# Transposed tokens through one PSUM bank, a third bank for the first layer, and a larger lead for routing steps: a mixture-of-experts kernel

## Chip, cores and metric

The kernel runs on one core of a Trainium2 chip. The metric is device time in microseconds (us), the median of three runs. Everything is one launch: a short causal convolution, the routing of its rows to eight experts, and the experts' two-layer networks.

## What is computed

```python
# x (8, 3584, 192) f32, weight (8, 7); w_gate (192, 8), w1 (8, 192, 1024), w2 (8, 1024, 192)
attn = 7-tap causal convolution of x along the sequence, one softmaxed filter per 24 channels
x = attn.reshape(28672, 192);  cap = 28672 // 8
logits = x @ w_gate
for idx in np.argsort(-logits.flatten()):     # greedy: best (token, expert) pairs first
    ...                                       # a token takes its first expert with room (cap 3584)
for e in range(8):
    mask = assigned == e
    out[mask] = np.maximum(x[mask] @ w1[e], 0.0) @ w2[e]
```

All data are float32. The kernel multiplies in float32r and splits an operand into a rounded part ("hi", names ending in h) and the rest ("lo", names ending in l), and adds the products that matter.

## The kernel before

**Stages.** Up to about 205 us the kernel computes the convolution in 16 pieces, the logits, and a first threshold. From then to the end it runs the experts' networks in `FFN.run`, one tile of 512 tokens after another, 56 tiles in all. Routing isn't finished when the experts start: the first 8 tiles (one per expert) hold tokens that a high threshold has already settled, the next 16 tiles need the list `ia`, tiles 24 to 26 need the list `ib0`, and the rest need `ib`. The routing that makes these lists is written as Python generators that yield between small steps, and it is woven into the experts' instructions while the program is built.

**One tile.** Iteration `i` of `FFN.run` has eight steps `f`. Step `f` issues, in this order: the first layer of tile `i` for hidden units `128 f` to `128 f + 127` (`l1`: five matmuls into one bank of the PSUM pool `ph`, a Relu on ScalarE to `hh`, and on VectorE the difference `hl`), a call of the routing hook, one preparation step for tile `i + 1` (`prep`), half a block of the second layer of tile `i - 1` (`l2`: eight matmuls into a bank of the pool `py`; after every second half `store`, with a Copy on ScalarE, an add on VectorE and an indirect DMA issued by GpSimd), the hook again, and one piece of weight splitting (`wsplit`). The hook is also called in the middle of `l1` and of `l2`, four times a step in all. A tile thus has 40 matmuls of the first layer and 64 of the second.

**Preparing a tile.** The 512 rows of a tile are gathered two iterations ahead into `xg` (`gather`, GpSimd's queue). They have to be transposed. While routing is still going on, TensorE does it: `prep` calls `transp` at steps 2 and 3. `transp(i, 0)` takes two of the four blocks of 128 tokens and `transp(i, 1)` the other two; each block has one transpose of its first 128 channels into the bank `pa` and one of the last 64 into the bank `pd`. Steps 4 and 5 (`evac`) take `pa` and then `pd` out: a Copy to the rounded part on ScalarE and a subtraction on VectorE, into `xa` and `xd`. Once no routing step is left (`free()`), a later tile is transposed on VectorE instead, by `shuffle`, in 16 instructions.

**Banks.** PSUM has eight banks of 512 f32 here: two for routing (`bg`), two for `py`, two for `ph`, and one each for `pa` and `pd` (pool `pt`, one buffer for each of two names).

**How far routing runs ahead.** `Pace` keeps three running totals while the program is built, `pe`, `dve` and `act`: the time that each engine's instructions would take by fixed charges. `Steps.hook` puts in up to four routing steps, and stops as soon as the next step has to wait for a product of TensorE that is not due yet (`need`), or VectorE's total is more than `slack` ahead of TensorE's, or ScalarE's more than `act` ahead. In the experts' stage the two limits are `SS = (0.65, 2)`. A step that needs a TensorE result first yields `PEW` or `PEA`, which sets `need` to 0.8 us after the total of VectorE (or of VectorE and ScalarE).

**Where routing must be finished.** `idx_of`, called by `gather` for tile `i + 2`, puts in all steps that are still missing for the list it needs (`drain`). For tile 24 it is `bg.drain(1)` in iteration 22, ahead of that iteration's first matmul: everything in `rest()`, whose last parts are `final` and `lists`. All engines work through their instructions in program order, so the expert matmuls of that iteration stand behind the drained steps.

Of the kernel before, what the change touches and what calls it, by code (L numbers as in the profile page):

```python
# [5 lines left out]
F32 = mybir.dt.float32  # L6
# [6 lines left out]
PSUM = bass.MemoryType.PSUM  # L13

NE, D, NTOK, F, CAP = 8, 192, 28672, 1024, 3584
# [96 lines left out]
def build(ctx, tc, nc, x, weight, wg, attn, LT, wk):  # L112
# [147 lines left out]
    def logits_t(i):  # L260
# [10 lines left out]
        if not last:  # L271
            V.tensor_tensor(o, o, v[:, 1], op=OP.add)

    k.load, k.conv, k.transp, k.split, k.logits, k.logits_t = load, conv, transp, split, logits, logits_t
    k.toeplitz, k.gate_ops, k.transp_last, k.logits_last = toeplitz, gate_ops, transp_last, logits_last
    return k
# [808 lines left out]
class FFN:  # L1085
# [122 lines left out]
                in_offset=bass.IndirectOffsetOnAxis(ap=idx[b], axis=0),  # L1208
                bounds_check=rows - 1, oob_is_err=False)

    def transp(self, i, u):

        x = self.XG[i]
        if u == 0:
            self.pa = self.pt.tile([128, 512], F32, name="pa")
            self.pd = self.pt.tile([128, 512], F32, name="pd")
        for b in (2 * u, 2 * u + 1):
            q = slice(128 * b, 128 * b + 128)
            self.nc.tensor.transpose(self.pa[:, q], x[:, b, 0:128], self.ident)
            self.nc.tensor.transpose(self.pd[0:64, q], x[:, b, 128:D], self.ident)  # L1220
        if u:
            self.XG.pop(i)

    def evac(self, i, u):

        A, V = self.nc.scalar, self.nc.vector
        if u == 0:
            self.XT[i] = (self.xs.tile([128, 2, 512], FR, name="xa"), self.xs.tile([128, 512], FR, name="xd"))
        xa, xd = self.XT[i]
        hi, lo, p = ((xa[:, 0], xa[:, 1], self.pa), (xd[0:64], xd[64:128], self.pd[0:64]))[u]  # L1230
        A.activation(hi, p, AF.Copy)
        V.tensor_tensor(lo, p, hi.bitcast(F32), op=OP.subtract)

# [76 lines left out]
    def prep(self, i, step):  # L1310

        if i in self.free:
            if step < 7:
                self.shuffle(i, step)
            return
        if step == 2 or step == 3:
            self.transp(i, step - 2)
        elif step == 4 or step == 5:
            self.evac(i, step - 4)

    def run(self, idx_of, at, eng, free):

# [29 lines left out]
def moe_kernel(ctx, tc, x, weight, wg, w1, w2, out):  # L1352
# [6 lines left out]
    with ExitStack() as cw:  # L1359
        pool = lambda c, name, bufs, **kw: c.enter_context(tc.tile_pool(name=name, bufs=bufs, **kw))  # L1360
        late = dict(reuse_waits="tile")
        right = dict(side="right")
# [5 lines left out]
        r = Route(tc, nc, LT, lst, wk, drm)  # L1368
        r.oh_pool = oh
        r.bg = lambda: bgp.tile([128, 512], F32, name="bg")  # L1370
        ff = FFN(tc, nc, attn, w1, w2, out, r.ident, wr, drm)
# [128 lines left out]
        cx[0].close()  # L1500
        cc.close()
        ff.pt = pool(cw, "pt", 1, space=PSUM, **right, **late)
        ff.ph = pool(cw, "ph", 2, space=PSUM, **right, **late)
        bg.drain(5)
        nc.lat, nc.las = (0.8, 1.2)
        gather()
        bg.keep = 0
        ff.xs = pool(cw, "fx", 2, **late)
        for u in range(2):
            ff.transp(0, u)  # L1510
        for u in range(2):
            ff.evac(0, u)
        for _ in range(2):
            ff.wsplit(-1, P)
# [26 lines left out]
                bg.drain()  # L1541
            return [ib[:, e, 4 * (t - 3) + b:4 * (t - 3) + b + 1] for b in range(4)]

        SS = (0.65, 2)
        ff.bg = lambda: bg.hook(SS[0], 4, SS[1])

        def at(i):
# [41 lines left out]
```

## Time and profile before

| | us |
|---|---|
| median of 3 runs | 1375.17 (1374.98 to 1376.15) |
| the profiled execution: its own time | 1377.14 |
| its span, first to last instruction | 1375.2 |
| TensorE busy, matmuls | 1288.4 (94%) |
| VectorE busy | 1046.1 (76%) |
| ScalarE busy | 586.0 (43%) |
| GpSimd busy | 637.0 (46%) |
| mean granted TensorE clock | 0.964 of full speed |

The profiled execution took 1.9 us more than its span, and 2.0 us more than the median. In the views that follow PE is TensorE's matmuls, PEld its weight loads, DVE is VectorE, ACT ScalarE, POOL GpSimd. `ph<-xa,w` is an instruction that writes `ph` and reads `xa` and `w`. A stretch of the view by windows gives, after its length, for each engine the busy time and (x) the number of instructions. In the waits an idle time of an engine is put down to what came last before the waiting instruction began; "issue" means that the profile shows nothing that it waited for.

### The profile page before, as it was taken

The page shows a single profiled execution, that of the slowest core. Times are in us where ns is not written, and L with a number is a line of the kernel's source. Part 1 is how long each engine was busy: PE and PEld are TensorE (multiplying, and loading weights), DVE is VectorE, ACT ScalarE, POOL GpSimd, SP SyncE. Part 2 cuts the span into 40 slices and gives each one's busy share as a digit, 9 for nine tenths or more (in the row PEclk, how much of TensorE's full clock was granted, in tenths as well). Part 3 has the DMA queues.
Part 4 walks back from the last instruction along what each step waited for, and adds up shares of the span by engine and source line. Part 5 has one row for each costly group of instructions (what it writes and reads, how often), then busy time and mean ns, then how long its engine had stood idle before and what let it go on. Part 6 is the DMA issues. An engine that isn't in the chain of part 4 may idle for free.

```text
span 1375.2 us, 20862 instructions
## 1 busy us (share of the span) xinstructions
PE 1288.4 (94%) x7367; PEld 1106.8 (80%) x7367; DVE 1046.1 (76%) x2216; ACT 586.0 (43%) x1242; POOL 637.0 (46%) x607
## 2 busy tenths in 40 slices
PE   5978897998989999999959999999999999999997
PEld 2545564887879989889848999999999999999997
DVE  7598963777988888888877477777777777777772
ACT  4755473447544434434413433333333333333332
POOL 5655566556754443443403344444444444444432
PEclk9998897999999999999959999999999999999999
DMA  9996568677872443343312152324231414141110
GB/s 231 284 271 166 170 218 286 204 231 248 260 260 83 143 137 97 138 143 118 100 60 81 32 197 89 101 89 139 86 99 49 140 44 146 45 142 42 42 35 28
DMA packets 114431, 188.23 MB, mean 137 GB/s; under 512 B 12352, under 2 KB 86544, under 8 KB 110096
## 3 DMA queue, kind: packets, MB, share of 16 engines
q1 hardware_dynamic: 63888, 120.75, 27.6%
q0 software_dynamic: 21504, 44.07, 10.3%
q10 hardware_dynamic: 28928, 22.02, 4.9%
q8 instruction: 59, 0.97, 0.3%
q14 instruction: 52, 0.43, 0.1%
HBM read 114.44 MB, written 72.35 MB: 136 GB/s over the span
## 4 chain that ended last, share of the span: by engine, by line
PE 74%; DVE 14%; DMA 4%; issue 3%; ACT 2%; POOL 2%; SPq 0%; POOLq 0%; DVEq 0%; ACTq 0%
PE ph L53 34%; PE y L53 32%; PE bg L53 4%; DVE X L53 4%; DMA attn<-a 2%; DVE oa L53 2%; DVE aT L53 2%; PE cv L53 1%; DVE hl L53 1%; DMA raw<-in_moe_w_dram 1%; POOL xg L1206 1%; PE pl L53 1%; DVE TH L53 1%; PE pd L53 1%; ACT hi L53 1%
## 5 line engine op out<-in xcount | busy, mean ns | idle before, releaser
L53 PE MATMUL y<-w,hh 128*128 128x384 f32 x1792 | 541.7, 358 | 0.0
L53 ACT ACTIVATE hh<-ph 128x512 fp32r<-128x512 f32 x448 | 267.7, 598 | 508.7 <-PE ph L53 377.6
L53 DVE SCALAR_TENSOR_TENSOR hl<-ph,hh 128x512 fp32r<-128x512 f32 x448 | 308.5, 689 | 196.6 <-ACT hh L53 163.7
L53 PE MATMUL y<-w,hl 128*128 128x192 f32 x1792 | 450.3, 251 | 0.0
L53 PE MATMUL ph<-xa,w 128*128 128x512 f32 x1344 | 401.7, 407 | 17.3 <-DVE hl L53 13.3
L53 PEld LDWEIGHTS y<-w,hl 128*128 128x128 f32 x1792 | 342.8, 191 | 15.4
L53 PEld LDWEIGHTS y<-w,hh 128*128 128x128 f32 x1792 | 338.4, 189 | 17.1
L1274 POOL DMA_INDIRECT out_dram<-yo,ib x128 | 126.9, 992 | 294.9 <-DVE yo L53 279.5
L53 PEld LDWEIGHTS ph<-xa,w 128*128 128x128 f32 x1344 | 221.4, 191 | 42.2 <-DVE hl L53 16.4
L1274 POOL DMA_INDIRECT out_dram<-yo,ia x96 | 107.4, 1118 | 240.6 <-DVE yo L53 202.6
L53 DVE STREAM_TRANSPOSE xs<-xg 32x256 f32<-32x256 f32 x480 | 176.9, 369 | 8.3
L53 PE MATMUL ph<-xd,w 128*128 128x512 f32 x448 | 179.2, 400 | 0.0
L53 PE MATMUL ph<-xd,dl 128*128 128x512 f32 x448 | 176.0, 393 | 0.0
L1206 POOL DMA_INDIRECT xg<-attn,ib x128 | 130.1, 1016 | 70.2 <-issue 69.9
L226 POOL TENSOR_TENSOR lo<-aT,hi 128x768 fp32r<-128x768 f32 x50 | 93.3, 1896 | 73.5 <-ACT hi L53 73.5
L53 PE MATMUL cv<-X,TH 118*128 118x384 f32 x256 | 106.6, 548 | 19.2 <-DVE TH L53 12.8
L1206 POOL DMA_INDIRECT xg<-attn,ia x96 | 105.2, 1096 | 28.8 <-issue 27.6
L53 ACT ACTIVATE yt<-y 128x192 f32<-128x192 f32 x224 | 73.4, 328 | 97.5 <-PE y L53 87.5
L53 DVE TENSOR_TENSOR yo<-y,yt 128x192 f32<-128x192 f32 x224 | 79.6, 355 | 45.6 <-ACT yt L53 42.4
L53 PEld LDWEIGHTS cv<-X,TH 118*128 118x128 f32 x256 | 50.4, 210 | 65.2 <-issue 14.8
L53 PEld LDWEIGHTS ph<-xd,w 128*128 128x128 f32 x448 | 85.2, 190 | 21.3 <-issue 2.2
L53 PEld LDWEIGHTS ph<-xd,dl 128*128 128x128 f32 x448 | 85.1, 190 | 19.9 <-POOL dl L1187 0.3
(241 smaller groups left out, 1233.5 us busy)
## 6 DMA issues: line engine op xcount, KB each, us to landing
w<-kw SPq DMA_DIRECT2D x16, 1536.0 KB
w<-kv SPq DMA_DIRECT2D x16, 1536.0 KB
X<-in_x_dram SPq DMA_DIRECT2D x16, 1344.0 KB
attn<-a ACTq DMA_DIRECT2D x16, 1344.0 KB
kw<-w SPq DMA_DIRECT2D x48, 256.0 KB
kv<-w SPq DMA_DIRECT2D x32, 384.0 KB
raw<-in_moe_w_dram SPq DMA_DIRECT2D x32, 192.0 KB
raw<-in_moe_w_dram SPq DMA_DIRECT2D x16, 256.0 KB
```

The lines of the kernel that those rows point to most:

```text
L53: return f(*a, **k)
L226: eng.tensor_tensor(lo, aT, hi.bitcast(F32), op=OP.subtract)
L1206: self.nc.gpsimd.indirect_dma_start(out=t[:, b], out_offset=None, in_=self.attn[0:rows], in_offset=bass.IndirectOffsetOnAxis(ap=idx[b], ax ...
L1274: st = nc.gpsimd.indirect_dma_start(out=self.out, out_offset=bass.IndirectOffsetOnAxis(ap=idx, axis=0), in_=o, in_offset=None, bounds_chec ...
```

## The change

Three things change together.

1. `transp` transposes all four blocks of one half of the channels at a time: part 0 the first 128 channels, part 1 the last 64. Both parts use one name, `px`, so the pool `pt` holds one bank instead of two. `prep` calls them at steps 1 and 4, and `evac` at steps 2 and 5. For the first tile, ahead of the loop, the second part goes to a routing bank.
2. The freed bank goes to the first layer: `ph` has three.
3. `SS` goes from (0.65, 2) to (1.8, 3): routing steps may stand up to 1.8 us ahead on VectorE and 3 us on ScalarE.

```diff
-    def transp(self, i, u):
+    def transp(self, i, u, bank=None):
         x = self.XG[i]
-        if u == 0:
-            self.pa = self.pt.tile([128, 512], F32, name="pa")
-            self.pd = self.pt.tile([128, 512], F32, name="pd")
-        for b in (2 * u, 2 * u + 1):
+        p = self.px = bank or self.pt.tile([128, 512], F32, name="px")
+        for b in range(4):
             q = slice(128 * b, 128 * b + 128)
-            self.nc.tensor.transpose(self.pa[:, q], x[:, b, 0:128], self.ident)
-            self.nc.tensor.transpose(self.pd[0:64, q], x[:, b, 128:D], self.ident)
+            if u == 0:
+                self.nc.tensor.transpose(p[:, q], x[:, b, 0:128], self.ident)
+            else:
+                self.nc.tensor.transpose(p[0:64, q], x[:, b, 128:D], self.ident)
...
-        hi, lo, p = ((xa[:, 0], xa[:, 1], self.pa), (xd[0:64], xd[64:128], self.pd[0:64]))[u]
+        hi, lo, p = ((xa[:, 0], xa[:, 1], self.px), (xd[0:64], xd[64:128], self.px[0:64]))[u]
...
-        if step == 2 or step == 3:
-            self.transp(i, step - 2)
-        elif step == 4 or step == 5:
-            self.evac(i, step - 4)
+        if step in (1, 4):
+            self.transp(i, step // 4)
+        elif step in (2, 5):
+            self.evac(i, step // 5)
...
-        ff.ph = pool(cw, "ph", 2, space=PSUM, **right, **late)
+        ff.ph = pool(cw, "ph", 3, space=PSUM, **right, **late)
...
         for u in range(2):
-            ff.transp(0, u)
-        for u in range(2):
+            ff.transp(0, u, r.bg() if u else None)
             ff.evac(0, u)
...
-        SS = (0.65, 2)
+        SS = (1.8, 3)
```

## The prediction

> **What bounds the kernel now.** First the slices of the page, 34.4 us each, to see which engine is full and where it isn't.
>
> ```profile
> PE   5978897998989999999959999999999999999997
> DVE  7598963777988888888877477777777777777772
> PEclk9998897999999999999959999999999999999999
> ```
>
> From the seventh slice on, where the experts run, TensorE is the full engine, with one hole: the 21st slice, about 688 to 722 us, at half busy and half clock. VectorE is at 8 tenths in the slices before it, and at 7 in it and (but for one 4) after it. So the end is set by TensorE's queue, and what is to be won is time in which that queue stands or is fed badly. To size it I cut the trace at tile starts (the first Relu of a tile), the drain itself once more, and one tile without any routing of each kind.
>
> ```profile
> core 0: us, PE busy (x) PEld busy (x) DVE busy (x) ACT busy (x) POOL busy (x), PEclk, DMA share, GB/s
> 385.90:411.90 26.00, 21.57 (x112) 18.77 (x113) 22.28 (x54) 8.79 (x19) 12.55 (x13) 0.87 0.71 245
> 411.90:669.80 257.90, 256.85 (x1511) 230.68 (x1511) 220.32 (x522) 113.04 (x278) 113.45 (x104) 1.00 0.36 120
> 669.80:723.10 53.30, 38.58 (x324) 33.72 (x324) 41.49 (x108) 12.15 (x23) 10.30 (x10) 0.71 0.23 79
> 690.00:723.00 33.00, 19.28 (x208) 16.73 (x209) 24.93 (x66) 5.07 (x9) 1.97 (x2) 0.54 0.14 47
> 723.10:773.50 50.40, 49.76 (x398) 44.73 (x398) 35.14 (x75) 18.18 (x34) 15.15 (x16) 1.00 0.18 62
> 773.50:792.70 19.20, 19.20 (x114) 17.42 (x113) 8.15 (x14) 6.99 (x15) 8.06 (x9) 1.00 0.22 69
> 811.00:829.30 18.30, 18.30 (x106) 16.61 (x105) 13.95 (x30) 7.12 (x15) 7.90 (x8) 1.00 0.63 229
> ```
>
> A tile without transposes on TensorE takes 18.3 us (its 104 matmuls, and two counted at the edges), one with them 19.2 us. One step `f` is therefore 18.3 / 8 = 2.29 us. Against 19.2 the other rows show what routing costs. The row of 53.3 us is one tile (324 matmul records, of which 211 write `bg`, by the row below). It is 34.1 us too long. In the 33 us inside it TensorE is busy 19.28 us at a clock of 0.54, VectorE 24.93 us: that is `bg.drain(1)` of iteration 22, where the matmuls of a whole tile stand behind the rest of the routing.
>
> ```profile
> 411.90:669.80 257.90, 7.73 (x53) 3.55 (x35) 7.26 (x34) 0.00 (x0) 1.00 0.36 120
> 669.80:723.10 53.30, 18.36 (x211) 1.37 (x11) 3.66 (x12) 5.07 (x9) 0.71 0.23 79
> 693.66 0.26 PE L53 MATMUL bg<-ones,F 128*128 128x1 bf16 x4 [4.67 <-DVE F L53]
> 704.25 0.91 PE L53 MATMUL bg<-X,oa 128*128 128x16 bf16 x10 [6.37 <-DVE oa L53]
> 722.19 1.04 POOL L1206 DMA_INDIRECT xg<-attn,ib  x1 [30.08 <-issue]
> ```
>
> (The windows again for instructions on `bg` alone, then three rows of the timeline.) The two long waits of TensorE in the drain end with VectorE's `F` and `oa`, both steps of `rest()`; the gather that needed the list comes out of GpSimd's queue 30.08 us after its last one. So the drain is a VectorE chain, and TensorE has nothing else to do.
>
> **Part 1, the larger lead: what it removes.** Not all of the 34.1 us can go, since the drained steps also have TensorE work. Its price where it is hidden can be read: the stretch of 50.4 us is two tiles (398 records less 2 x 112, so 174 of routing, the last list) with TensorE busy 49.76 us, and it is 50.4 - 38.4 = 12.0 us too long. For 211 instead of 174 such matmuls that makes 12.0 x 211 / 174 = 14.6 us. At most 34.1 - 14.6 = 19.5 us can go.
>
> It goes only if VectorE does the drain's work earlier, about 24 of the 24.93 us (the rest is the last few `hl` and `yo` of the tile). Has it room? In the 13 tiles before (1511 records less 53, over 112) VectorE idles 257.9 - 220.32 = 37.6 us. What ended that idle time, and the same for the tiles before those:
>
> ```profile
> DVE hl L53 <- ACT hh L53: 20.5, 36, 1.4
> DVE hl L53 <- issue: 5.5, 8, 1.4
> DVE yo L53 <- ACT yt L53: 2.2, 5, 0.6
> DVE r_x L53 <- PE bg L53: 1.5, 2, 0.7
> DVE r_oki L53 <- PE bg L53: 0.7, 1, 0.7
> ...
> DVE hl L53 <- ACT hh L53: 29.1, 19, 6.6
> ```
>
> (Waits of VectorE from 411.9 to 669.8 us; the last row is that of 205 to 411.9.) 20.5 + 5.5 = 26 us is VectorE standing at `hl`, whose Relu isn't done. With a lead of 0.65 us the queue ahead of `hl` is empty by the time that the last matmuls of `l1` and the Relu are through; with 1.8 us there is still a routing step in it. That is the kind of idle time that a longer lead fills. Waits for a product of routing itself, which no lead removes, are 1.5 + 0.7 us in these rows. From 205 to 411.9 us the same kind is 29.1 us, but in part at the start, before there are steps to put in, with single waits up to 6.6 us; I count a third, 10 us. Room 36 us, need 24: two thirds have to be filled. I take it that nearly all of the drain goes and a stall of 3 us is left: 19.5 - 3 = 16.5 us gained; bounds 5 (a third filled) and 19.5.
>
> A routing list that ends earlier also lets `free()` turn earlier: each tile moved from `transp` to `shuffle` saves 19.2 - 18.3 = 0.9 us. I take one tile; bounds none and two, 0 to 1.8 us.
>
> **Part 2, the third bank of `ph`.** The waits of TensorE from 205 to 411.9 us:
>
> ```profile
> PE ph L53 <- DVE hl L53: 13.3, 9, 3.3
> PE bg L53 <- DVE r_cc L53: 1.4, 1, 1.4
> ...
> PE bg L53 <- DVE r_c L53: 1.0, 2, 0.5
> ```
>
> (The last row is from 411.9 to 669.8.) With two banks `l1` of step f + 2 waits until `hl` of step f has read its bank; with three, that of f + 3, one step or 2.29 us later. Nine waits of at most 3.3 us, 13.3 in all, would nearly vanish if VectorE were no later than now. But it will be fuller, and a VectorE that is late for good is only met a step later. Bounds 0 and 13.3 us, I take 4. After 411.9 us no wait for `hl` is listed, so there it gains nothing and only covers the larger lead.
>
> **Part 3, the one bank `px`.** The number of transposes stays.
>
> ```profile
> L53 PE MATMUL pa<-ident,xg x104: 270/272/421, 203.9 to 780.8; 128*128 128x128 f32 x104
> L53 ACT ACTIVATE xa<-pa x26: 589/592/610, 205.3 to 784.0; 128x512 fp32r<-128x512 f32 x26
> L53 DVE TENSOR_TENSOR xa<-pa,xa x26: 668/681/692, 205.9 to 784.8; 128x512 fp32r<-128x512 f32 x26
> ...
> L53 DVE TENSOR_TENSOR xd<-pd,xd x26: 683/685/686, 206.6 to 787.2; 64x512 fp32r<-64x512 f32 x26
> ```
>
> 26 tiles, four each for `pa` and for `pd`, before as after. New is a wait: the second half's transposes (step 4) need both readers of the first (step 2) to be done. Between stand two steps, 4.58 us; Copy and subtraction take 0.59 + 0.68 = 1.27, so VectorE and ScalarE may together be 3.3 us late. Behind the waiting transpose stand `l2` of the tile before and the next `l1`, all of TensorE. The next tile's first half comes four steps, 9.2 us, after the second's readers, and the readers themselves run three or more steps ahead of the next tile's `l1`. The trace shows no such wait. It costs nothing while VectorE is less than 3.3 us late, and can't gain; up to 5 us if that happens in some tiles. I take 1. The routing bank that the first tile borrows has no user then: nothing.
>
> **What the lead costs.** A VectorE without idle time doesn't catch up. The routing matmuls that wait for it (`r_cc`, `r_c`: 1.4 and 1.0 us in the rows above) may each become a little longer, and all expert matmuls stand behind them. From nothing to 12 us over 21 tiles; near those rows, I take 2. `yo` gets later as well, and with it GpSimd's stores, with the gathers behind them in its queue; those are for two tiles later, 38 us, and so hidden. ScalarE's limit of 3 delays Relus by up to 1 us more, which the third bank's 2.29 us cover.
>
> **The sum.** -16.5 - 0.9 - 4 + 1 + 2 = -18.4 us. The profiled execution took 1377.1 us (span 1375.2), which gives 1358.7; the median was 2.0 us below that execution, so 1356.7, rounded to 1357.
>
> **The rivals.** *The drain stays for its half*, because routing is held up by its round trips to TensorE rather than by the 0.65 us. For it: the seven rounds have some 30 places that yield for TensorE's results. Against: the waits on `bg` are 2.2 us beside 26. Then part 1 gives 8 us, no tile leaves `transp`, and the sum is -8 - 4 + 1 + 2 = -9: 1366.
>
> *VectorE loses its new work to GpSimd.* These rows are the same instruction twice, and GpSimd at the time of the second.
>
> ```profile
> 309.83 1.22 DVE L53 TENSOR_TENSOR LT<-LT,c_mu 128x1024 f32<-128x1024 f32 x1
> 312.16 3.15 DVE L53 TENSOR_TENSOR LT<-LT,c_mu 128x1024 f32<-128x1024 f32 x1
> 311.95 2.26 POOL L1187 TENSOR_TENSOR w<-raw,w 128x384 fp32r<-128x384 f32 x2
> ```
>
> Under GpSimd's weight splitting it took 1.93 us longer. The splitting runs until about 402 us; with 10 us more of such work there, some 20 instructions of half a us, and a quarter of them met, VectorE loses 5 x 1.93 = 10 us: room 26 for a need of 24. The drain then goes by half at best and the third bank's gain is eaten: -8 + 1 + 1 = -6, so 1369. The Trainium skill states this as a rule ("SBUF — State Buffer", section "Who interferes with whom"): VectorE with two inputs in SBUF and GpSimd share a port pair that one of them locks for a whole instruction, and the other waits. These rows agree (3.15 against 1.22 us). By that rule alone, without the row's overlap, a fuller VectorE can only be blocked more often before 402 us, and the sum would be nearer to 1369 than to 1357.
>
> *Slower: the lead turns into waits of TensorE.* In the tile of 385.9 to 411.9 us VectorE is 22.28 of 26 us busy, and the tile takes 26.0 instead of 19.2 us. If in each of the 21 tiles with routing TensorE meets VectorE late once more, at a routing product, at `px` or at `hl`, at the 1.4 us of the row for `r_cc`, that is 29 us: -18 + 29 = +11, so 1386. It decides from 18.4 / 21 = 0.9 us a tile. Against: the 13 tiles of the long row have VectorE 85% busy and TensorE still 256.85 of 257.9.
>
> *Nothing happens*: the limits aren't what holds the steps back, or what is won is given back: 1375.
>
> **Chances.** Forecast 0.66, with its own range 1346 (19.5 + 1.8 + 8 of the bank's waits, no cost) to 1363 (6 us more of cost or of drain left); the half drain 0.12; GpSimd 0.08; slower 0.10; nothing 0.04. About 0.2%, 2.8 us, is what a measurement of this kernel can tell from no change. Faster than that: 0.66 + 0.12 + 0.08 = 0.86; same 0.04; slower 0.10. The range 1346 to 1371 leaves out the slower case, the one without effect, and the tails of the forecast.
>
> **What would show it.** Right, if the tile that holds the drain (now 53.3 us) shrinks to about 37, with no stretch at a clock near 0.54 and no gather 30 us late, if VectorE is over 90% busy in the tiles before it and its waits at `hl` there fall from 26 to under 10 us, if `ph` waits for `hl` less than 13.3 us before 412 us, and if `xa<-px` and `xd<-px` occur 25 or 24 times. Part 3 is wrong if transposes show idle time before them that ends with VectorE's `xa`. The prediction is wrong if the 13 tiles of 19.8 us each grow by 0.9 us or more, or if the drain still leaves TensorE idle for over 10 us.

## The result, and the profile after

The changed kernel takes 1360.0 us (median of four runs, 1359.2 to 1360.9) against 1375.7 for the kernel before in the same measurement: a ratio of 0.9886, 95% interval 0.9872 to 0.9900, or 15.6 us less. 1357 was predicted, in a range of 1346 to 1371. The profiled execution's span went from 1375.2 to 1357.9 us, 17.3 us less. It differs from the 15.6 us because the profiled execution of the kernel before took 1.5 us more than the median given here, and that of the changed kernel 0.3 us less than its own. (In other sessions the kernel before came out at 1375.2 to 1379.2 us, so the runs below are compared by their ratio to it.)

The slices of the page of the changed kernel, 33.9 us each:

```profile
span 1357.9 us, 20887 instructions
...
PE   5878896999889999999999999999999999999997
...
DVE  7698964777999898898775777777777777777772
...
PEclk9988898999989999999989999999999999999999
```

TensorE's hole in the 21st slice is gone, and with it the half clock. VectorE is at 8 or 9 tenths from the 11th to the 19th slice and mostly at 7 from the 20th: routing ends earlier. The stretches, cut again at the first Relu of a tile: tile 0, tiles 1 to 7, 8 to 18, then 19, 20, 21, 22 and 23 one by one, with the columns explained before the prediction.

```profile
212.60:241.70 29.10, 22.79 (x77) 13.00 (x77) 9.04 (x15) 10.60 (x20) 16.92 (x17) 0.89 0.84 281
241.70:410.90 169.20, 154.99 (x995) 135.78 (x994) 144.25 (x288) 92.51 (x221) 102.99 (x91) 0.97 0.72 236
410.90:631.70 220.80, 219.56 (x1293) 196.07 (x1292) 200.02 (x497) 95.72 (x234) 95.15 (x89) 1.00 0.37 123
631.70:653.10 21.40, 21.21 (x145) 18.67 (x145) 19.49 (x44) 7.44 (x16) 8.94 (x8) 1.00 0.35 117
653.10:685.20 32.10, 32.10 (x294) 28.61 (x293) 23.64 (x58) 11.47 (x21) 9.87 (x8) 0.95 0.22 77
685.20:719.20 34.00, 33.05 (x276) 29.78 (x275) 22.59 (x47) 11.41 (x20) 9.44 (x8) 0.90 0.26 88
719.20:738.40 19.20, 19.20 (x115) 17.39 (x113) 10.09 (x24) 7.08 (x14) 8.16 (x9) 1.00 0.35 111
738.40:756.70 18.30, 18.30 (x106) 16.61 (x106) 14.04 (x30) 7.04 (x14) 7.96 (x9) 1.00 0.34 124
```

The last two routing lists now lie in tiles 20 and 21 (294 and 276 matmul records where a tile has 112), and TensorE is busy through nearly all of both. Above the 19.2 us of a tile they cost 12.9 and 14.8 us. Before, the drain's tile and the two after it cost 34.1 + 12.0 = 46.1 us; now 27.7, 18.4 us less. Tiles 23 and 24 no longer transpose on TensorE: 1.8 us less. In the other direction, tiles 8 to 19 take 242.2 us, 11.8 above twelve times 19.2, where tiles 8 to 20 were 8.3 us above: 3.5 us more. Tiles 1 to 7 take 169.2 us; the same tiles were 241.1 to 411.9 us before, 170.8: 1.6 us less. They start 0.6 us later. In all -18.4 - 1.8 + 3.5 - 1.6 + 0.6 = -17.7 us by the end of tile 24, and what follows is 0.4 us longer.

VectorE's idle time at `hl`, from 410.9 to 631.7 us (tiles 8 to 18):

```profile
DVE hl L53 <- ACT hh L53: 13.2, 18, 2.0
DVE yo L53 <- ACT yt L53: 1.3, 3, 0.6
```

In 11 tiles it idles 220.8 - 200.02 = 20.8 us, 1.9 a tile, against 37.6 us in 13 tiles, 2.9 a tile. In tiles 1 to 7 its idle time fell from 32.5 to 25.0 us, again about 1.0 a tile. This idle time is where the drained steps went. What TensorE waits for from 205 to 410.9 us has changed hands:

```profile
PE bg L53 <- DVE r_cc L53: 6.8, 2, 5.6
PE bg L53 <- ACT oa L53: 4.3, 1, 4.3
...
PE ph L53 <- DVE hl L53: 3.2, 2, 1.7
PE px L53 <- DVE xa L53: 2.5, 3, 1.3
```

The waits of `l1` for `hl` fell from 13.3 to 3.2 us; waits of 5.6 and 4.3 us for routing products are new, and so are 2.5 us at the one bank `px`. All rows of this view come to 22.0 us before and 24.4 us now, so in this stretch TensorE doesn't wait less. The 5.6 us has a cause of its own. Two of VectorE's routing rows occur twice within 10 us, and the second time each takes over three times as long:

```profile
369.02 1.09 DVE L53 TENSOR_TENSOR X<-r_w,m_f 128x896 bf16<-128x896 f32 x1
...
370.89 1.01 DVE L53 TENSOR_TENSOR X<-X 128x448 bf16<-128x448 bf16 x3
...
375.15 3.67 DVE L53 TENSOR_TENSOR X<-r_w,m_f 128x896 bf16<-128x896 f32 x1
...
379.01 3.74 DVE L53 TENSOR_TENSOR X<-X 128x448 bf16<-128x448 bf16 x3
```

GpSimd at that time, and TensorE behind it:

```profile
375.88 1.99 POOL L1187 TENSOR_TENSOR w<-raw,w 128x384 fp32r<-128x384 f32 x2
...
380.40 2.23 POOL L1187 TENSOR_TENSOR w<-raw,w 128x384 fp32r<-128x384 f32 x2
...
383.10 0.20 PE L53 MATMUL bg<-r_cc,ones 128*128 128x56 bf16 x1 [5.60 <-DVE r_cc L53]
```

Both long rows lie over subtractions of weight parts on GpSimd. They delay `r_cc`, the routing matmul stands in TensorE's queue for it, and the expert matmuls behind it stand too. So the gain is there, by the drain, while one of the rivals is at work in tiles 1 to 7. The experiments take the three edits apart first, and that rival next.

### The profile page after: what moved, and what is told of

Read it like the earlier page. It is cut to its first block, busy times and chain, and to the rows that moved or that the text cites. A ratio compares the mean times of both kernels' runs of the same rounds, so it can differ in the third digit from the quotient of the medians.

```text
span 1357.9 us, 20887 instructions
## 1 busy us (share of the span) xinstructions
PE 1282.5 (94%) x7351; PEld 1099.0 (81%) x7351; DVE 1055.2 (78%) x2248; ACT 587.7 (43%) x1242; POOL 636.1 (47%) x607
## 4 chain that ended last, share of the span: by engine, by line
PE 73%; DVE 15%; DMA 4%; issue 3%; POOL 2%; ACT 2%; SPq 0%; POOLq 0%; DVEq 0%; ACTq 0%
PE ph L53 34%; PE y L53 33%; DVE X L53 4%; PE bg L53 3%; DMA attn<-a 2%; DVE aT L53 2%; DVE oa L53 2%; DVE hl L53 1%; PE cv L53 1%; DMA raw<-in_moe_w_dram 1%; POOL w L1187 1%; PE px L53 1%; DVE TH L53 1%; POOL xg L1206 1%; ACT hi L53 1%
## 5 line engine op out<-in xcount | busy, mean ns | idle before, releaser
L53 DVE STREAM_TRANSPOSE xs<-xg 32x256 f32<-32x256 f32 (+1 forms) x512 | 188.8, 369 | 8.8
L1206 POOL DMA_INDIRECT xg<-attn,ia x96 | 108.7, 1133 | 28.8 <-issue 24.3
L53 PEld LDWEIGHTS cv<-X,TH 118*128 118x128 f32 x256 | 51.2, 213 | 65.5 <-issue 14.6
```

The source lines that it names most:

```text
L53: return f(*a, **k)
L1206: self.nc.gpsimd.indirect_dma_start(out=t[:, b], out_offset=None, in_=self.attn[0:rows], in_offset=bass.IndirectOffsetOnAxis(ap=idx[b], ax ...
```

## Experiments

### The three edits, one or two at a time

The lead alone:

```diff
-        SS = (0.65, 2)
+        SS = (1.8, 3)
```

> The kernel before with the larger lead (1.8, 3) alone: banks pa and pd, two banks of ph, transposes at steps 2 and 3. Theory (the gain is the drained list, filled in earlier; the banks only cover lateness): routing ends as early as in the changed kernel, 24 tiles transposed on TensorE, no stretch at half clock, but l1 meets a late hl more often than with three banks: some 5 us slower than the changed kernel, about 1365. Rival (without the third bank a lead of 1.8 us turns into TensorE waits that eat the gain): 1372 or more, with over 20 us of waits for hl. Rival (banks count for nothing): 1360.

Measured: 1366.6 us, ratio 0.9901 (0.9880 to 0.9923). By its ratio that is 12.5 us less than before, between the 10 of the theory (1365) and the 15 of the rival in which banks count for nothing (1360). The interval holds the rival and ends just short of the theory, so this run doesn't decide between them. Two banks of `ph` keep the waits for `hl` from 205 to 412 us as large as they were before the change:

```profile
PE ph L53 <- DVE hl L53: 12.8, 10, 2.2
...
PE bg L53 <- DVE r_cc L53: 4.8, 1, 4.8
```

So the other rival falls: the lead doesn't turn into 20 us of waits, and by itself brings most of the gain.

The banks without the lead: the changed kernel with `SS = (0.65, 2)`.

> The changed kernel with the old lead (0.65, 2): one bank px, three banks of ph. Theory: the drain of iteration 22 stays at about 53 us for its tile, waits of l1 for hl before 412 us shrink from 13.3 to under 5 us, the time is 0 to 4 us below the kernel before: 1373. Rival (the third bank carries the gain): under 1368. Rival (px costs): over 1377.

Measured: 1368.9 us, ratio 0.9922 (0.9902 to 0.9943), 10 us less than before. The theory had 0 to 4 us; by its size it is what the rival named that lets the third bank carry the gain (under 1368, over 7 us less). But it isn't the third bank alone, as the next run shows. It is the same with two banks of `ph`, so that the one bank `px`, with its new places for `transp` and `evac`, is all that is changed:

```diff
-        SS = (1.8, 3)
+        SS = (0.65, 2)
...
-        ff.ph = pool(cw, "ph", 3, space=PSUM, **right, **late)
+        ff.ph = pool(cw, "ph", 2, space=PSUM, **right, **late)
```

> The one bank px alone, with the old lead and two banks of ph: one PSUM bank stays empty. It takes apart the run that kept the old lead, which gained 10 us where 0 to 4 were expected. Theory: the new place of transp and evac lets the planner fit routing steps in earlier, and this doesn't need the third bank, so 8 us below the kernel before, with the tile of the drain at about 47 us. Rival (the third bank gave it, by fewer waits for hl): within 4 us of the kernel before.

Measured: 1370.3 us, ratio 0.9964 (0.9951 to 0.9978), 5 us less, between the theory's 8 and the rival's 4. The stretches of that run for the tile of the drain and the two that follow:

```profile
669.10:715.70 46.60, 36.12 (x315) 32.05 (x314) 37.30 (x90) 12.13 (x23) 10.28 (x10) 0.76 0.26 89
715.70:768.00 52.30, 51.66 (x398) 46.18 (x398) 34.94 (x75) 18.28 (x35) 15.62 (x16) 0.95 0.18 59
```

The drain's tile takes 46.6 instead of 53.3 us, with 37.30 instead of 41.49 us of VectorE's work: some routing steps moved ahead of it although the lead is the old one. The rest of the 10 us, between the two runs, goes with the third bank: 0.9922 against 0.9964 in different sessions, whose intervals nearly touch, and 1366.8 against 1368.9 us of profiled span. Under the old lead it comes out at 2 to 6 us. How much of that is the bank's own isn't shown: in tiles 1 to 7 VectorE is busy 146.87 us with two banks and 142.26 with three, for 275 instructions in both, so the first run also met more of the hold-ups that are dealt with below.

Under the new lead it was tried twice, the second time beside the changed kernel itself.

```diff
-        ff.ph = pool(cw, "ph", 3, space=PSUM, **right, **late)
+        ff.ph = pool(cw, "ph", 2, space=PSUM, **right, **late)
```

> The changed kernel with two banks of ph instead of three, and px alone (one PSUM bank stays empty). Theory: as the lead alone, about 1365, and px by itself adds less than 1 us to that. Rival (px's wait matters): 3 us or more over the run with the lead alone.

Measured: ratio 0.9887 (0.9866 to 0.9909), 1363.1 us. That is no slower than the changed kernel's 0.9886, and 3.5 us faster than the lead alone in the same session, where the theory had no difference; the two intervals overlap over most of their length.

> The changed kernel once more, to stand beside the run of this call with two banks of ph. Expected: 0.9886 of the kernel before, 1360.

> The changed kernel with two banks of ph, beside the changed kernel itself. Theory (the third bank takes up lateness before 412 us, as it did with the old lead): 2 to 5 us slower than the changed kernel in this call. Rival (what it saves in waits for hl turns up as other waits): within 1.5 us of it.

Measured in one session: 1361.7 us, 0.9898 (0.9878 to 0.9917), with three banks; 1362.1 us, 0.9903 (0.9883 to 0.9922), with two. The rival holds: the difference is 0.4 us, well inside the intervals. Yet the waits for `hl` differ much. With two banks, from 205 to 412 us:

```profile
PE ph L53 <- DVE hl L53: 13.5, 11, 3.2
PE bg L53 <- DVE r_cc L53: 5.0, 1, 5.0
...
PE bg L53 <- ACT oa L53: 0.7, 1, 0.7
```

and with three in the same session:

```profile
PE bg L53 <- DVE r_cc L53: 6.8, 2, 5.6
PE bg L53 <- ACT oa L53: 4.6, 1, 4.6
...
PE bg L53 <- DVE oa L53: 2.8, 3, 1.5
PE ph L53 <- DVE hl L53: 2.8, 2, 1.7
```

10.7 us of waits for `hl` vanish, and TensorE then waits 3.9 us longer for VectorE's `r_cc` and `oa`, and another 3.9 us longer for ScalarE's `oa`. All rows come to 23.8 us with two banks and 22.4 us with three. Tiles 1 to 7 differ by 1.4 us in all:

```profile
241.30:414.60 173.30, 158.49 (x993) 140.18 (x993) 146.52 (x294) 93.57 (x221) 104.56 (x91) 0.95 0.73 235
```

with two banks, and with three:

```profile
239.60:411.50 171.90, 158.48 (x995) 139.66 (x994) 145.14 (x288) 92.41 (x221) 102.50 (x91) 0.95 0.72 233
```

VectorE is 84% busy in both. The third bank lets TensorE start its next matmuls earlier while VectorE is late, and what it then meets is the next thing that VectorE or ScalarE is late with.

### A lead of 3 us

```diff
-        SS = (1.8, 3)
+        SS = (3.0, 3)
```

> The changed kernel with a lead of 3 us instead of 1.8. Theory (the drain is gone already, the rest is routing's own TensorE work, and a later VectorE only makes TensorE wait): 0 to 6 us slower than the changed kernel. Rival (idle VectorE time still holds routing back): 3 us or more faster.

Measured: 1356.6 us, ratio 0.9862 (0.9847 to 0.9877). The theory had the same or slower, the rival 3 us or more faster. Against the changed kernel's two measurements, 0.9886 and 0.9898, it is 3 to 5 us faster; but it was measured in a session of its own, and its interval overlaps the first of the two and nearly reaches the second, so that isn't settled. In its profile the two last lists lie one tile earlier again, in tiles 19 and 20:

```profile
628.90:663.30 34.40, 33.73 (x294) 30.21 (x293) 25.19 (x59) 11.68 (x22) 10.55 (x8) 0.90 0.23 78
663.30:700.30 37.00, 36.15 (x276) 32.07 (x275) 23.44 (x50) 11.36 (x20) 9.92 (x8) 0.82 0.20 66
```

They cost 15.2 and 17.8 us there, 5.3 us more than with a lead of 1.8, so a later VectorE does begin to cost TensorE something.

### GpSimd's subtractions

These two leave out part of the computation: where GpSimd would subtract, it writes zeros, so the products with the small parts of the weights are missing. Routing doesn't use them.

```diff
-        eng.tensor_tensor(lo, r[0:n], hi[0:n].bitcast(F32), op=OP.subtract)
+        if eng is self.nc.gpsimd:
+            eng.memset(lo.bitcast(F32), 0.0)
+        else:
+            eng.tensor_tensor(lo, r[0:n], hi[0:n].bitcast(F32), op=OP.subtract)
```

In the changed kernel:

> The changed kernel, but GpSimd writes zeros instead of subtracting when it splits weights, so the small parts of those weights are left out of the products; routing doesn't use them. GpSimd then reads no SBUF in these instructions. Theory (VectorE instructions with two SBUF inputs are held up while GpSimd's subtraction reads): the 3.67 and 3.74 us instructions before 402 us fall back to about 1.1, the wait of 5.6 us for r_cc goes, and the time is 5 to 9 us lower: about 1353. Rival (they are long for another reason): within 2 us of the changed kernel's 1360.

Measured: 1343.7 us, ratio 0.9738 (0.9717 to 0.9759): 20 us off the changed kernel, over twice the 5 to 9 us that were expected. The same VectorE instruction over the whole run, with its shortest, median and longest duration in ns, first of the changed kernel:

```profile
L53 DVE TENSOR_TENSOR X<-r_w,m_f x10: 1091/1158/3670, 369.0 to 553.9; 128x960 bf16<-128x960 f32 x8, 128x896 bf16<-128x896 f32 x2
```

and with GpSimd only writing:

```profile
L53 DVE TENSOR_TENSOR X<-r_w,m_f x10: 1092/1158/1160, 358.2 to 537.0; 128x960 bf16<-128x960 f32 x8, 128x896 bf16<-128x896 f32 x2
```

No long one is left, and the wait of 5.6 us for `r_cc` is gone. Writing zeros is also shorter than subtracting (0.44 against 1.03 us in the median), so that alone could have made the two meet less often. But the instruction that took 3.67 us lies over two of these writes here, and isn't held up:

```profile
364.26 1.09 DVE L53 TENSOR_TENSOR X<-r_w,m_f 128x896 bf16<-128x896 f32 x1
...
364.42 0.79 POOL L1188 MEMSET w<- 128x384 f32 x2
```

In the kernel before:

> The kernel before, with the same omission as the run that left the subtraction out of the changed kernel: GpSimd writes zeros in place of the small parts of the weights. Theory (the hold-ups cost the larger lead more, since a fuller VectorE meets more of them): it gains less than the changed kernel does, some 8 us against 16, and stays 20 us or more above 1344. Rival (they cost both alike): 16 us below the kernel before. Rival (the change's own gain is less room lost to GpSimd): the two kernels without the subtraction are within 8 us of each other.

Measured: 1355.2 us, ratio 0.9850 (0.9835 to 0.9865), 20.6 us less. So the theory that the fuller VectorE meets more hold-ups is wrong in its size: they cost both kernels about 20 us. And without them the change brings 0.9850 to 0.9738, 1.1%, which is what it brings with them; so the third account, by which the two kernels would then be within 8 us of each other, falls as well.

If GpSimd's reads are what costs, the work can go to VectorE, with nothing left out:

```diff
-        VP = (1, 3)
+        VP = (0, 1, 2, 3, 4, 5, 6, 7)
```

In the changed kernel:

> The changed kernel with every weight subtraction on VectorE while routing runs, none on GpSimd: 48 more instructions of 0.45 to 0.67 us there, some 25 us of work, in exchange for the hold-ups. Theory: VectorE has about that much room before 412 us, so the waits for r_cc go, but the lists end later: between 1350 and 1358. Rival (VectorE becomes the bound in these tiles): 1365 or more.

Measured: 1342.1 us, ratio 0.9760 (0.9747 to 0.9773). It beats both kernels, by 1.3% and 2.4%, and the forecast of 1350 too. Tiles 1 to 7 of its profile, and the longest of the instruction above:

```profile
240.80:390.80 150.00, 148.71 (x990) 133.33 (x989) 131.72 (x293) 89.62 (x205) 60.92 (x52) 1.00 0.84 275
```

```profile
L53 DVE TENSOR_TENSOR X<-r_w,m_f x10: 1092/1157/1200, 384.4 to 557.8; 128x960 bf16<-128x960 f32 x8, 128x896 bf16<-128x896 f32 x2
```

150.0 instead of 169.2 us, TensorE nearly without a hole and at full clock. VectorE does all the subtractions of these tiles and is still only 88% busy; the lists end one tile later than in the changed kernel.

The same line in the kernel before:

> The kernel before with every weight subtraction on VectorE. Theory (hold-ups by GpSimd cost this kernel some 20 us as well, but its lead leaves less room for the subtractions, so the drain of iteration 22 gets longer): 5 to 12 us below the kernel before, against 18 for the changed kernel. Rival (the same gain in both): 18 us below it.

Measured: 1367.1 us, ratio 0.9949 (0.9931 to 0.9967), 7 us less, as expected. Its profile says where the rest went:

```profile
234.50:387.60 153.10, 152.03 (x994) 134.31 (x993) 122.17 (x251) 89.96 (x207) 58.30 (x51) 1.00 0.83 270
644.60:709.70 65.10, 39.53 (x325) 33.98 (x324) 54.50 (x139) 15.86 (x39) 9.83 (x10) 0.66 0.18 64
```

What the hold-ups took from VectorE can be read off the first part of its page, since nothing else is added or left out in this kernel:

```profile
PE 1284.1 (94%) x7367; PEld 1104.6 (81%) x7367; DVE 1049.2 (77%) x2262; ACT 587.8 (43%) x1242; POOL 584.6 (43%) x561
```

with the row of the new subtractions:

```profile
L53 DVE TENSOR_TENSOR w<-raw,w x46: 541/558/694, 210.8 to 378.0; 128x384 fp32r<-128x384 f32 x32, 128x512 fp32r<-128x512 f32 x14
```

46 of them at 0.56 us are 26 us more work, and VectorE is busy 1049.2 - 1046.1 = 3 us longer: about 23 us of its time before were hold-ups. The two runs that write zeros give, for the kernel before and the changed one, 1046.1 - 1028.3 = 17.8 and 1055.2 - 1031.5 = 23.7 us over the whole run, but 138.34 - 116.92 = 21.4 and 144.25 - 127.39 = 16.9 us in tiles 1 to 7. So the figure is good to some 6 us, and doesn't show that one kernel loses more. Tiles 1 to 7 are 17.7 us shorter than before, but the tile of the drain grows from 53.3 to 65.1 us: under the lead of 0.65 us the subtractions displace routing steps, which come back in the drain, 54.50 us of VectorE's time instead of 41.49. With the larger lead they find room. This is the clearest sign of what the lead does.

Last, both edits that were faster than the changed kernel:

> Subtractions on VectorE and a lead of 3 us, the two edits that were each faster than the changed kernel. Theory: what the longer lead gave was one more tile whose transposes leave TensorE, 0.9 us, and lists put in earlier; the gains add: 1336 to 1341. Rival (a lead of 3 us without hold-ups only makes VectorE late): 1342 or more.

Measured: 1347.1 us, ratio 0.9788 (0.9768 to 0.9807). The gains don't add; the rival holds, and 1.8 us with the subtractions on VectorE stays the fastest measured, though the intervals (0.9773 and 0.9768 at their near ends) just overlap.

## Why the prediction was right, and where not

**The drain.** 16.5 us were forecast; the lists' tiles became 18.4 us cheaper. Part of that is only a move: the lists' tiles now hold 40 routing matmuls fewer, and tiles 8 to 19 hold 39 more than tiles 8 to 20 did (records above 112 a tile). At 0.069 us each, the prediction's 12.0 us for 174, this is an estimated 2.7 us, which leaves some 15.7 us for the drain. The price of a hidden list, forecast at 14.6 us for 211 routing matmuls, was measured at 12.9 for 182 and 14.8 for 164. The room was judged rightly in kind: idle time at `hl` was what the lead filled, and the run with the lead alone together with the longer drain of the kernel that had the lead of 0.65 us and the subtractions on VectorE show that VectorE's filling, and not round trips to TensorE, set the drain's size. In size less of it was filled than thought: VectorE is 90.6% busy in tiles 8 to 19, as the prediction asked, but its waits at `hl` there fell from 26 to 14.2 us and not under 10, and from 205 us to the end of tile 7 they didn't fall (29.1 and 36.0 us). One stall of 3 us was to be left. There is none in one piece, but the 346 routing matmuls of the two lists' tiles would cost 23.9 us at 0.069 us each, an estimate, and cost 27.7, at a granted clock of 0.95 and 0.90. The gather that came 30 us late is no longer held up: no gather from 410.9 to 740 us waits over 0.3 us at "issue". Two tiles instead of one left `transp`, 1.8 for 0.9 us.

**The third bank.** 4 us were forecast within 0 to 13.3. The waits for `hl` did shrink as described, by about 10 us, but under the larger lead the time did not follow: 0.4 us between medians, 1.4 us in tiles 1 to 7. The sentence that "a VectorE that is late for good is only met a step later" was the right one, and the 4 us too many.

**The bank `px`.** Its wait was costed at 1 us, and transposes idle behind VectorE's `xa` were to be the sign that this part is wrong. They occur: 2.5 us in one profile of the changed kernel, 0.6 in the other, 4.2 with the old lead and three banks of `ph`. The step "can't gain" failed too: with the old lead and two banks of `ph` it gave 5 us. `evac` moved from steps 4 and 5 to 2 and 5, and the routing steps are placed by totals that include `evac`'s instructions; less routing was left for the drain (37.30 us of VectorE in its tile instead of 41.49). That the new spacing is the cause is argued from this; a run that moves `evac` and nothing else wasn't made. With the new lead `px` adds at most a little: 0.9901 without it, 0.9887 and 0.9903 with it.

**What the lead costs.** 2 us were forecast; tiles 8 to 19 became 3.5 us dearer. Of these, 2.7 us are the estimate for the routing matmuls that moved there, so what the lead itself costs in these tiles is about 1 us.

**The sum.** The parts come to -17.3 us of span where -18.4 was forecast. That it is so near is in part luck: the drain and the transposes gave 2.8 us more than was forecast, and the third bank, `px`, the lead and all the rest together 3.9 us less. The parts aren't additive: the lead alone gives 1.0%, both bank edits alone 0.8%, all together 1.1%. Both shorten the same thing, the steps that are left for the drain: its tile is 47.0 us long with the bank edits alone.

**The rivals.** The half drain and the slower case didn't happen: TensorE's tiles with routing grew by 3.5 us in 12, 0.3 us a tile, where 0.9 us in each of 21 was the point from which it decides. GpSimd's hold-ups are real, and in both kernels cost 20 us; the rival was wrong in that the change makes them dearer. Its rule from the Trainium skill ("SBUF — State Buffer", section "Who interferes with whom") has a second half: a VectorE instruction with two inputs in SBUF contends with a GpSimd instruction that reads SBUF, and not with one that only writes it. The trace agrees: the same instruction took 3.67 us over GpSimd's subtractions and 1.09 us over its writes of zeros. Two inputs aren't the whole of it, though: in the kernel before, a VectorE instruction with one tensor input (`r_dd<-r_d`, 128x8 f32), which takes 0.17 us elsewhere, took 2.74 us over two subtractions of GpSimd, at 394.47 us.

## What to carry to other kernels

Side work that is put in between the steps of a full engine should be sized by the idle time of the engine that does it, and by what that engine waits for: a lead shorter than the wait for the next operand leaves a hole at each step, and the holes come back in one piece where the work must be done. Edits that fill the same holes don't add up, so each is tried alone and with the others. Before an engine's work is handed to GpSimd to spare VectorE, its effect on VectorE's own instructions is measured: here VectorE could do 26 us of subtractions for 3 us of its time.

## What was unexpected in the hardware

A hold-up of VectorE can last longer than the one GpSimd instruction that it meets: the instruction at 375.15 us ended at 378.82, after GpSimd's two subtractions (375.88 to 377.87), which follow each other. It takes about as much from the kernel, 20 us in both, as from VectorE, some 20 us too, although VectorE isn't the full engine: TensorE waits behind a routing matmul, and its granted clock in tiles 1 to 7 is 0.97 with the hold-ups and 1.00 without.
